# Attention with an expert layer on one core: first x tiles in PSUM, the rare-case flag inside the plan, outputs in another order, no table of rank shifts, longer dense dummies

## The chip, the core and the metric

One core of a Trainium2 chip runs the whole program. The metric is the device time of one execution in microseconds (us), as the median of several. The engines are named as in the profile: PE (TensorE, matrix products, with PEld for its weight loads), DVE (VectorE), ACT (ScalarE), POOL (GpSimd) and SP (SyncE, which issues nearly all DMAs). A name with q behind it (SPq) is an engine's queue. Matrix products write PSUM banks of 512 fp32 columns; DVE and ACT can read them, POOL and DMAs can't.

## What is computed

```python
B, H, S, D = 4, 8, 768, 64            # n_sink 4, window 128
scores = matmul(q, k.T) / sqrt(D)
keep = is_sink | ((rel >= 0) & (rel < window))
a = softmax(where(keep, scores, -1e9))
x = matmul(a, v) -> [3072 tokens, 512]
gate = 1 / (1 + exp(-(x @ w_gate)))   # w_gate, w_val: 512 x 1536
val = x @ w_val
out = (gate * val) @ w_out            # w_out: 1536 x 512
```

Inputs of the expert layer's weights are 64-bit floats. The products of the expert layer keep fp32 accuracy by splitting each operand into a high part (rounded to fp32r) and the rest, and summing three products: high x high, high x rest, rest x high.

## The kernel before

**A planner orders everything.** The kernel builds a list of operations (`plan.op`), each with a priority, one or more engines that could run it with an estimated time, the tiles it reads and those it writes. `Plan.run` then plays a clock: whenever an engine is free, it takes the ready operation with the smallest priority, gives it its buffers, and appends it to that engine's instruction stream. `Tile` is a buffer drawn from a numbered set (`tag`, `bufs`); `plan.over` names sets that share memory, where a later one is given out only once all of the earlier are through. An operation's `slack` delays, in the plan, the moment at which its tiles come free. On PE an operation is *sure* only some time (`SURE` 600 ns, `SURE_D` 1200 ns after a DMA) after its last producer should end.

**Dummies.** When PE finds nothing, `Plan.run` may put in a dummy product (`warm`, of the identity with itself). While the planner's clock is under `DENSE`, operations that aren't sure are held back and a dummy is put in every time; after that an operation that isn't sure may run, and a dummy is put in only when PE's share of work lately is under `FLOOR`.

**Rank shifts.** `RANKS` is a table of 862 numbers. Just before the plan runs, a loop at the end adds to each operation's priority the number that stands for its engine and its group (attention operations by their step u, expert operations by their place in a chunk).

**Attention.** 24 tiles of 128 rows are taken two at a time (12 supertiles), each in four steps of two heads; u counts heads, 0 to 95. `attend` issues for each step: loads of k, q, v; scores on PE into two PSUM banks; masking and the row minimum on DVE (`pick`, `top`, the latter writing a column of `negm_all`), exp on ACT, normalising (`norm`) on POOL or DVE, four transposes on PE, a copy on ACT, a selection on POOL (`split`), and the product with the values on PE (`pv`, `pv_one` for the early steps) into a bank of the set AS (`a`, four banks, used for scores and transposes too). ACT copies that bank to a quarter of x in SBUF (`xr`, one tile for every two steps). After the fourth step `join` adds the sink columns: a PE product of `sk` and `vsp` into a fresh bank, a DVE addition onto xr, then `copy` rounds to `XH` and `rest` takes the difference `XL`, on DVE or POOL.

**Expert layer.** Tiles in `SPILL` go to DRAM for later. The other four supertiles run through `feed` (chunks ci = 0 to 3, 256 rows, 12 slices f of the hidden width) while attention goes on and the weights are decoded from their 64-bit form (`decode`, `weights`). The rest are four wide blocks of 512 rows (`wino`, ci = 4 to 7) that use seven products in place of eight: NP = 6 passes p, each with a gate and a value unit (`Unit`, steps `first` to `fourth`) and `downs`, which splits the hidden tile and queues seven products in the list `coming`. Those are run between the steps of the next pass: one after `first`, two each after `second`, `third` and `fourth`. PE runs the wide blocks in exactly the order in which their operations are listed (`pe_op`). `passing` products go through a rotating bank and are added to one of four accumulators in SBUF (`ACC`, profile name tf); `staying` products accumulate in PSUM over all passes. After the seventh product of the last pass, `merge` combines the accumulators and `emit` writes four outputs, each a DMA of 256 KB. The next block's accumulators are the same four buffers.

**The end.** After `plan.run` come the operations that decide whether the inputs were unusual (`bad`, `count`, `flag`, `total`), a load of that number on every engine, and a branch to `general`, which is not taken here. The last block takes another path through `downs` and `emit` (`last`).

The lines of the loops that matter, beside the functions below:

```python
for i in range(len(OS)): plan.over[f"o{i}", 0] = {("eO", i)}
MX = {3: MS, 2: [MS[0][:, 0:256], MS[1][:, 0:256], MS[1][:, 256:512]]}   # banks of the plain expert products, "m2"
DROPS = ((1, 2, 2, 2), (0, 2, 2, 3)) + ((1, 2, 2, 2),) * 4 + ((0, 1, 2, 4),)
```

In the profile nearly every instruction stands at line 677, since one helper (`InOrder`) records them all; they are told apart by their tiles' names.

## Time and profile before

| | |
|---|---|
| timed runs | 714.39, 716.55, 717.35 us; median 716.55 |
| the profiled execution | 718.86 us, of which 717.1 us are the span from first to last instruction |
| mean granted clock of PE | 0.996 of full speed |
| busy PE / DVE / ACT / POOL | 98% / 79% / 53% / 73% |
| DMA | 152.75 MB, mean 213 GB/s |

The rows below come from one profiled execution; times in them are us from the start of its span, or durations in us, and ns where a row says mean ns. A bracket at the end of a row of the timeline gives how long the engine sat idle before it and what released it. A matmul's busy time is its latency, so products that follow each other overlap in it.

### The profile page before, as it was taken

The page shows a single profiled execution, that of the slowest core. Times are in us where ns is not written, and L with a number is a line of the kernel's source. Part 1 is how long each engine was busy: PE and PEld are TensorE (multiplying, and loading weights), DVE is VectorE, ACT ScalarE, POOL GpSimd, SP SyncE. Part 2 cuts the span into 40 slices and gives each one's busy share as a digit, 9 for nine tenths or more (in the row PEclk, how much of TensorE's full clock was granted, in tenths as well). Part 3 has the DMA queues.
Part 4 walks back from the last instruction along what each step waited for, and adds up shares of the span by engine and source line. Part 5 has one row for each costly group of instructions (what it writes and reads, how often), then busy time and mean ns, then how long its engine had stood idle before and what let it go on. Part 6 is the DMA issues. An engine that isn't in the chain of part 4 may idle for free.

```text
span 717.1 us, 18023 instructions
## 1 busy us (share of the span) xinstructions
PE 700.7 (98%) x6488; PEld 649.7 (91%) x6488; DVE 570.0 (79%) x1296; ACT 381.4 (53%) x1052; POOL 522.2 (73%) x490
## 2 busy tenths in 40 slices
PE   8999899999999999999999999999899999999997
PEld 7778788888887888888999999999899999999996
DVE  8999989989895677875567798668888688886765
ACT  6898867754544565652453454543445444454431
POOL 3889867699997877764477697775768687786651
PEclk9999999999999999999999999999999999999999
DMA  9987879667776888855757656666467756665611
GB/s 291 295 245 257 289 235 311 233 211 251 245 246 193 273 264 264 283 143 173 233 178 227 185 163 202 210 220 186 154 182 216 227 184 176 184 206 183 187 50 64
DMA packets 110609, 152.75 MB, mean 213 GB/s; under 512 B 11060, under 2 KB 69428, under 8 KB 110516
## 3 DMA queue, kind: packets, MB, share of 16 engines
q1 hardware_dynamic: 110512, 151.56, 67.4%
q8 instruction: 52, 0.85, 0.5%
q14 instruction: 41, 0.34, 0.1%
q10 hardware_dynamic: 4, 0.00, 0.0%
HBM read 124.26 MB, written 27.26 MB: 211 GB/s over the span
## 4 chain that ended last, share of the span: by engine, by line
PE 77%; DVE 12%; DMA 4%; issue 3%; ACT 2%; POOL 1%; SPq 0%; DVEq 0%; POOLq 0%; ACTq 0%
PE a L677 38%; PE m L677 24%; PE o L677 15%; DVE tf L677 3%; DMA out_dram<-tf 2%; DVE w L677 2%; DVE a L677 1%; DVE tt L677 1%; DVE P L677 1%; DVE traw L677 1%; DMA wst<-in_moe_w_gate_dram 1%; DMA wst<-wol_d 1%; DVE XH L677 1%; DMA tf<-tw_d 1%; ACT P L677 1%
## 5 line engine op out<-in xcount | busy, mean ns | idle before, releaser
L677 POOL TENSOR_TENSOR tt<-tf,tt 128x512 fp32r<-128x512 f32 x75 | 103.3, 1389 | 26.9 <-ACT tt L677 11.6
L677 ACT ACTIVATE P<-P,negm_all 128x132 f32<-128x132 f32 x176 | 70.0, 399 | 23.7 <-DVE negm_all L677 23.4
L677 POOL TENSOR_SCALAR_AFFINE_SELECT wt<-wt 128x512 f32<-128x512 f32 (+1 forms) x88 | 63.1, 719 | 15.6 <-ACT wt L677 12.4
L677 PE MATMUL o<-woh,graw 128*128 128x512 f32 x192 | 74.1, 410 | 0.2 <-DVE graw L677 0.2
L677 ACT ACTIVATE tf<-a 128x512 f32<-128x512 f32 x49 | 29.3, 599 | 84.3 <-DVE a L677 62.3
L677 PE MATMUL m<-XH,wvh 128*128 128x256 f32 x216 | 61.6, 296 | 0.9 <-ACT traw L677 0.5
L677 ACT CAST tt<-tf 128x512 fp32r<-128x512 f32 x72 | 44.6, 620 | 27.9 <-PE a L677 21.8
L677 PE MATMUL m<-XH,wgh 128*128 128x256 f32 x193 | 56.5, 293 | 2.1 <-DVE traw L677 2.1
L677 PE MATMUL a<-xa,tt 128*128 128x256 f32 x360 | 57.2, 281 | 0.2 <-DVE a L677 0.2
L677 PE MATMUL m<-XH,wvl 128*128 128x256 f32 x204 | 57.4, 281 | 0.0
L677 PE MATMUL m<-XL,wvh 128*128 128x256 f32 x204 | 57.4, 281 | 0.0
L677 PE MATMUL m<-XH,wgl 128*128 128x256 f32 x192 | 54.4, 283 | 0.0
L677 PE MATMUL m<-XL,wgh 128*128 128x256 f32 x192 | 54.3, 283 | 0.0
L677 POOL TENSOR_TENSOR XH<-tf,XH 128x512 fp32r<-128x512 f32 x25 | 34.1, 1364 | 24.0 <-ACT XH L677 21.6
L677 PEld LDWEIGHTS a<-xa,tt 128*128 128x128 f32 x360 | 49.3, 188 | 0.5 <-DVE a L677 0.4
L677 POOL TENSOR_TENSOR XL<-tf,XL 128x512 fp32r<-128x512 f32 x14 | 18.2, 1303 | 41.2 <-ACT XL L677 41.2
L677 POOL TENSOR_TENSOR P<-P,rs 128x528 f32<-128x528 f32 x34 | 42.7, 1256 | 7.1 <-DVE rs L677 2.4
L677 PEld LDWEIGHTS m<-XH,wvh 128*128 128x128 f32 x216 | 40.0, 189 | 7.0 <-issue 2.9
L677 PEld LDWEIGHTS o<-woh,graw 128*128 128x128 f32 x192 | 36.1, 188 | 10.6 <-issue 3.7
L677 DVE TENSOR_TENSOR a<-a,big 128x256 f32<-128x256 f32 x72 | 30.4, 425 | 18.3 <-PE a L677 17.1
L677 PEld LDWEIGHTS m<-XH,wgh 128*128 128x128 f32 x193 | 36.7, 190 | 6.7 <-DVE traw L677 2.9
L677 DVE COPY_PREDICATED a<-tri,a 128x256 f32<-128x256 int32 (+1 forms) x90 | 30.7, 377 | 13.6 <-PE a L677 13.6
(409 smaller groups left out, 2647.1 us busy)
## 6 DMA issues: line engine op xcount, KB each, us to landing
tf<-tw_d SPq DMA_DIRECT2D x96, 256.0 KB, 3.2
wol<-wol_d SPq DMA_DIRECT2D x90, 256.0 KB, 3.5
qkT<-in_k_dram SPq DMA_DIRECT2D x30, 198.0 KB, 4.1
wgh<-tu_d SPq DMA_DIRECT2D x46, 128.0 KB, 2.7
wgl<-tu_d SPq DMA_DIRECT2D x46, 128.0 KB, 2.9
wvh<-tu_d SPq DMA_DIRECT2D x46, 128.0 KB, 2.6
wvl<-tu_d SPq DMA_DIRECT2D x46, 128.0 KB, 3.5
v<-in_v_dram SPq DMA_DIRECT2D x30, 192.0 KB, 3.6
```

Source lines behind the costliest of these rows:

```text
L677: return lambda *a, **kw: tc.keep_in_program_order(op(*a, **kw))
```

## The change

DENSE goes from 8500 to 16000 (ns of the planner's clock). The table RANKS and the loop that adds it are gone. For the first supertile (two tiles of 128 rows, `DIRECT`) the four value products write into two PSUM banks that are kept (`eM`, which is the second m bank, and one of the set AS), `straight` lets the sink product accumulate there, and rounding and difference read the bank; the expert products get the second m bank only after that (`plan.over["m2", ...]`). At the end of the three inner wide blocks the sixth product is run before the fifth, and outputs leave after the third, fifth, sixth and seventh product in place of all after the seventh; an output's DMA holds its tile 1500 ns longer in the plan (`HOLD`). The flag's operations become operations of the plan, behind the last `top` of attention by their inputs and last in priority among attention's; `OUTP` only gives a name to the 0.5.

```diff
--- before.py
+++ after.py
@@ -40,7 +40,7 @@
 FLOOR = 0.85
-DENSE = 8500.0
+DENSE = 16000.0
 HEAT = 7000.0
@@ -78,6 +78,9 @@
 SPLIT = 6
+DIRECT = 1
+HOLD = 1500.0
+OUTP = 0.5
 B_xr = 3
@@ -95,133 +98,6 @@
 BUFS = {}
-RANKS = dict(
...
-)
 
...
@@ -806,6 +683,8 @@
         plan.over[f"o{i}", 0] = {("eO", i)}
+    for i in (1, 2):
+        plan.over["m2", i] = {("eM", 0)}
 
...
@@ -1099,7 +984,7 @@
                     [sc[e]] + [(MASKS, x) for x in ((0,), (1, 4), (2, 4))[min(t0 + t, 2)]],
-                    [(P, (e, t))],
+                    [(P, (e, t)), (NEGM, (u, e, t))],
                 )
@@ -1166,12 +1051,21 @@
 
+        direct = n_of[b, t0] < DIRECT
         if h % 4 == 0:
-            XS.append(Tile(XR_, None, F32, "xr", 3))
+            if not direct:
+                XS.append(Tile(XR_, None, F32, "xr", 3))
+            elif u == 0:
+                XS.append(Tile(MS[1:], None, F32, "eM", 1))
+            else:
+                XS.append(Tile(AS, None, F32, "a", len(AS)))
         xst, c = XS[-1], h // 2 % 2
         sides = [Tile(AS, None, F32, "a", len(AS)) for _ in range(2 - one)]
+        if direct:
+            sides = [xst]
 
@@ -1195,13 +1089,15 @@
 
+        home = c * W if direct else 0
+
         def pv_one():
                     PE.matmul(
-                        sides[0]()[e * D : e * D + D, c0 : c0 + n], lhsT=vt()[:, e, l],
+                        sides[0]()[e * D : e * D + D, home + c0 : home + c0 + n], lhsT=vt()[:, e, l],
                         rhs=w()[:, e].rearrange("p t x y -> p (t x y)")[:, r0 : r0 + n],
-                        start=i == 0, stop=i == len(wide) - 1, skip_group_check=True,
+                        start=i == 0 and not home, stop=i == len(wide) - 1, skip_group_check=True,
                         tile_position=(0, e * D),
@@ -1238,12 +1134,13 @@
                 )],
-                [vt, wt] + list(r), sides + [(xst, c)] + list(w), parts=True,
-            )
-            plan.op(
-                u, [("A", act(W, True), lambda: A.copy(out=xs()[:, c], in_=sides[0]()[:, 0:W]))],
-                [sides[0]], [(xst, c)],
-            )
+                [vt, wt] + list(r), sides + [(xst, c)] * (not direct) + list(w), parts=True,
+            )
+            if not direct:
+                plan.op(
+                    u, [("A", act(W, True), lambda: A.copy(out=xs()[:, c], in_=sides[0]()[:, 0:W]))],
+                    [sides[0]], [(xst, c)],
+                )
             if not one:
@@ -1256,6 +1153,32 @@
         return rear
+
+    def straight(u, g, T, XS, sk, runs):
+
+        W, vs = T * 128, VSP
+        k = g % RING * 128
+        for i, acc in enumerate(XS):
+
+            def add(i=i, acc=acc):
+                for c in range(2):
+                    PE.matmul(
+                        acc()[:, c * W : c * W + W], lhsT=vs()[:, 2 * i + c], rhs=sk(),
+                        start=False, stop=True, skip_group_check=True,
+                    )
+
+            plan.op(u, [("PE", 2 * mac(W), add)], [vs, sk], [acc])
+            x = lambda acc=acc: acc().rearrange("p (c x) -> p c x", c=2)
+            hi, lo = (lambda i=i, z=z: z()[:, 2 * i : 2 * i + 2, k : k + W] for z in (XH, XL))
+            parts = [(2 * i + c, (g + t) % RING) for t in range(T) for c in range(2)]
+            plan.op(
+                u, [
+                    ("A", act(2 * W, True), lambda x=x, hi=hi: A.copy(out=hi(), in_=x())),
+                    ("V", vec(2 * W), lambda x=x, hi=hi: V.tensor_copy(out=hi(), in_=x())),
+                ], [acc], [(XH, p) for p in parts],
+            )
+            rest(u, 2 * W, lo, x, hi, [acc] + [(XH, p) for p in parts], [(XL, p) for p in parts], True)
 
@@ -1297,6 +1220,9 @@
                 runs.append([t])
+        if n_of[b, t0] < DIRECT:
+            straight(u, g, T, XS, sk, runs)
+            return
         for i, xst in enumerate(XS):
@@ -2133,19 +2059,27 @@
         if p == NP - 1:
-            fourth = coming.pop()
-
-            def done():
-                fourth()
-                merge(ci, sums)
-                for n in range(4):
-                    emit(ci, g, n, O[n] if n < 3 else None, sums[n], False)
-
-            coming.append(done)
+            def also(n, *then):
+                product = coming[n]
+
+                def made():
+                    product()
+                    for x in then:
+                        x()
+
+                coming[n] = made
+
+            out_of = lambda n: lambda: emit(ci, g, n, O[n] if n < 3 else None, sums[n], False)
+            order = (0, 1, 2, 3, 5, 4, 6)
+            coming[:] = [coming[x] for x in order]
+            also(2, out_of(0))
+            also(4, lambda: merge(ci, sums), out_of(3))
+            also(5, out_of(2))
+            also(6, out_of(1))
 
 
-        pr = -1000.0 + ci + 1 - 0.5 / NP
+        pr = -1000.0 + ci + 1 - OUTP / NP
         last = ci == len(MT) + WT - 1
@@ -2157,7 +2091,7 @@
     def emit(ci, g, n, bank, acc, last):
-        pr = -1000.0 + ci + 1 - 0.5 / NP
+        pr = -1000.0 + ci + 1 - OUTP / NP
         r = home_of[1][g + n // 2 * 2] * 128
@@ -2186,7 +2120,7 @@
                 in_=ot()[:, 0:512].rearrange("p (j d) -> p j d", j=2),
-            ), [ot],
+            ), [ot], slack=HOLD,
         )
@@ -2248,40 +2182,40 @@
         feeds()
+    one = keep.tile([128, 1], F32, name="one")
+    nc.vector.memset(one, 1.0)
+    flag = keep.tile([1, 4], I32, name="flag")
+    total = keep.tile([1, 1], I32, name="total")
+    count = Tile(AS, None, F32, "a", len(AS))
+
+    def odd_values():
+        V.tensor_reduce(out=bad[:, 0:1], in_=negm_all, axis=AX.X, op=ALU.max)
+        V.tensor_scalar(
+            out=bad[:, 0:1], in0=bad[:, 0:1], scalar1=1.0e8, scalar2=None, op0=ALU.is_gt
+        )
+        for i, (x, y, op) in enumerate(
+            ((win, 1.0, ALU.is_lt), (win, float(WIN), ALU.is_gt), (nsk, float(NS), ALU.is_gt))
+        ):
+            V.tensor_scalar(out=bad[:, i + 1 : i + 2], in0=x, scalar1=y, scalar2=None, op0=op)
+
+    def counted():
+        PE.matmul(count()[0:1, 0:4], lhsT=one, rhs=bad, start=True, stop=True)
+
+    def decided():
+        V.tensor_copy(out=flag, in_=count()[0:1, 0:4])
+        V.tensor_reduce(out=total, in_=flag, axis=AX.X, op=ALU.max)
+
+    plan.op(B * NT * H // 2 + 1.0, [("V", 900, odd_values)], [NEGM], [FLAG])
+    plan.op(B * NT * H // 2 + 1.0, [("PE", 200, counted)], [FLAG], [count])
+    plan.op(B * NT * H // 2 + 1.0, [("V", 400, decided)], [count], [FLAG])
+
     ci = state["ci"]
         wino(ci + i, 4 * i)
-    for o in plan.ops:
-        e, pr = o.ways[0][0][0], o.prio
-        if 0 <= pr < 100:
-            o.prio += RANKS.get(e, {}).get(round(pr * 100), 0.0)
-        elif -1000.5 < pr < -900:
-            o.prio += RANKS.get("m" + e, {}).get(round((pr + 1000) * 12), 0.0)
-        elif 10000 <= pr < 11000:
-            o.prio += RANKS.get("M", {}).get(round((pr - 10000) * 24), 0.0)
     plan.run(WARM, 218.0, warm)
 
-    bad = keep.tile([128, 4], F32, name="bad")
...
-    V.tensor_reduce(out=total, in_=flag, axis=AX.X, op=ALU.max)
     main.close()
     flagged = nc.values_load(total[0:1, 0:1], min_val=0, max_val=512)
```

## Rows read from the trace of the kernel before

**Rows 1.** Page, part 1: busy us, share of the span, instructions.
```profile
PE 700.7 (98%) x6488; PEld 649.7 (91%) x6488; DVE 570.0 (79%) x1296; ACT 381.4 (53%) x1052; POOL 522.2 (73%) x490
```

**Rows 2.** Stretches: length, then busy us (instructions) of PE, PEld, DVE, ACT, POOL.
```profile
0.00:33.65 33.65, 31.03 (x289) 24.66 (x289) 30.31 (x117) 24.02 (x79) 18.87 (x33) 1.00 0.92 297
33.65:100.00 66.35, 64.16 (x591) 52.61 (x589) 62.28 (x196) 57.68 (x184) 56.35 (x57) 0.97 0.79 251
100.00:344.00 244.00, 242.27 (x2581) 212.63 (x2580) 195.32 (x592) 131.42 (x449) 189.01 (x203) 1.00 0.75 238
344.00:711.82 367.82, 363.01 (x3032) 359.76 (x3030) 280.49 (x384) 168.30 (x343) 258.00 (x198) 1.00 0.60 183
```

**Rows 3.** Dummies: their group (busy, mean ns), then two bursts in the timeline.
```profile
L677 PE MATMUL m<-ident 128*128 128x128 f32 x100 | 16.5, 322 | 1.8 <-POOL ident masks.py:199 1.8
...
1.76 4.21 PE L677 MATMUL m<-ident 128*128 128x128 f32 x18 [1.76 <-POOL ident masks.py:199]
...
12.46 2.05 PE L677 MATMUL m<-ident 128*128 128x128 f32 x16
```

**Rows 4.** PE's wait near 87 us, and the stretch after it (granted clock third from last).
```profile
88.80 0.39 PE L677 MATMUL m<-XH,wgh 128*128 128x256 f32 x1 [1.86 <-DVE traw L677]
...
88.00:94.00 6.00, 5.20 (x39) 4.26 (x40) 4.33 (x17) 4.05 (x14) 3.07 (x5) 0.72 0.73 240
```

**Rows 5.** Timeline around the first join: start us, us, engine, line, operation.
```profile
26.84 0.87 PE L677 MATMUL a<-wt,v 128*64 128x256 f32 x8
27.64 0.94 PE L677 MATMUL m<-ident 128*128 128x128 f32 x6
...
30.00 0.69 DVE L677 TENSOR_TENSOR xr<-o,xr 128x512 f32<-128x512 f32 x1
30.21 0.94 PE L677 MATMUL m<-ident 128*128 128x128 f32 x6
...
31.56 1.28 PE L677 MATMUL m<-ident 128*128 128x128 f32 x10
31.58 1.27 POOL L677 TENSOR_TENSOR XL<-xr,XH 128x512 fp32r<-128x512 f32 x1
...
33.65 0.39 PE L677 MATMUL m<-XH,wgh 128*128 128x256 f32 x1
```

**Rows 6.** Prices, from the groups by form: busy us, mean ns, idle before.
```profile
L677 ACT COPY xr<-a 128x256 f32<-128x256 f32 x48 | 17.7, 369 | 10.7 <-PE a L677 10.6
L677 DVE TENSOR_TENSOR xr<-a,xr 128x512 f32<-128x512 f32 x22 | 15.0, 682 | 2.3 <-PE a L677 2.1
L677 DVE TENSOR_TENSOR XL<-xr,XH 128x512 fp32r<-128x512 f32 x2 | 1.4, 714 | 0.0
L677 DVE CAST XH<-traw 128x512 fp32r<-128x512 f32 x4 | 2.1, 527 | 0.7 <-POOL traw L677 0.6
```

**Rows 7.** Timeline of the end, and the last output DMAs (us to landing).
```profile
711.86 0.76 DVE L677 SCALAR_TENSOR_TENSOR tf<-o,tf 128x256 f32<-128x256 f32 x2 [0.73 <-PE o L677]
...
712.31 0.82 SPq L677 DMA_DIRECT2D out_dram<-tf  x2
...
713.72 0.14 DVE L677 TENSOR_REDUCE total<-flag 1x1 int32<-1x4 int32 x1
...
out_dram<-tf SPq DMA_DIRECT2D x2, 128.0 KB, 1.8
```

**Rows 8.** Borders of wide blocks: chain of waits (first row), then timeline.
```profile
454.02 5.05 DMA out_dram<-tf
...
459.09 0.60 ACT L677 ACTIVATE tf<-o 128x512 f32<-128x512 f32 x1 [1.86 <-DMA out_dram<-tf]
...
459.74 0.38 PE L677 MATMUL o<-wvh,XL 128*128 128x256 f32 x1 [1.08 <-ACT tf L677]
...
552.74 0.38 PE L677 MATMUL m<-wvh,XL 128*128 128x256 f32 x1 [0.35 <-ACT tf L677]
...
644.10 0.39 PE L677 MATMUL o<-wvh,XL 128*128 128x256 f32 x1 [0.23 <-ACT tf L677]
```

More of the change, by code (lines that the diff above doesn't have):

```diff
@@ L775 @@
     READY, ready = Fixed(None), iter(range(1000))
+    NEGM, FLAG = Fixed(None), Fixed(None)
     AS = [ps.tile([128, 512], F32, name=f"a{i}") for i in range(B_a)]
@@ L815 @@
     val = keep.tile([128, 2], F32, name="val")
+    bad = keep.tile([128, 4], F32, name="bad")
     nsk, win = val[:, 0:1], val[:, 1:2]
@@ L949 @@
     ))])
+    cleared = []
     for i in range(len(OS) + BUFS["a"]):
@@ L958 @@
         ], w=[x])
+        cleared.append(x)
+    plan.op(SCALP, [("G", 60, lambda: G.memset(bad[:, 3:4], 0.0))], cleared)
     plan.op(SCALP, [("V", 530, scalars)], w=[nums])
@@ L969 @@
     place, home_of, n = {}, ([], []), 0
+    n_of = {}
     for b in range(B):
@@ L974 @@
             place[b, t0] = n in SPILL, len(to)
+            n_of[b, t0] = n
             to += range(b * NT + t0, b * NT + t0 + T)
@@ L1174, in attend @@
         sides = [Tile(AS, None, F32, "a", len(AS)) for _ in range(2 - one)]
+        if direct:
+            assert one and T == 2 and not place[b, t0][0]
+            sides = [xst]
         blocks = []
@@ L1258, in attend @@
         return rear
+    def straight(u, g, T, XS, sk, runs):
+        W, vs = T * 128, VSP
+        assert runs == [[0, 1]]
+        k = g % RING * 128
[17 more added lines that the diff above has]
+            rest(u, 2 * W, lo, x, hi, [acc] + [(XH, p) for p in parts], [(XL, p) for p in parts], True)
     def join(u, b, t0, T, XS, psk):
@@ L2253 @@
         wino(ci + i, 4 * i)
-    for o in plan.ops:
-        e, pr = o.ways[0][0][0], o.prio
-        if 0 <= pr < 100:
-            o.prio += RANKS.get(e, {}).get(round(pr * 100), 0.0)
-        elif -1000.5 < pr < -900:
-            o.prio += RANKS.get("m" + e, {}).get(round((pr + 1000) * 12), 0.0)
-        elif 10000 <= pr < 11000:
-            o.prio += RANKS.get("M", {}).get(round((pr - 10000) * 24), 0.0)
     plan.run(WARM, 218.0, warm)
     wres = {f: [w() if i < 4 else w()[:, 0] for i, w in enumerate(ws)] for f, ws in wres.items()}
-    bad = keep.tile([128, 4], F32, name="bad")
-    V.tensor_reduce(
-        out=bad[:, 0:1], in_=negm_all, axis=AX.X, op=ALU.max
-    )
-    V.tensor_scalar(
-        out=bad[:, 0:1], in0=bad[:, 0:1], scalar1=1.0e8, scalar2=None, op0=ALU.is_gt
-    )
-    for i, (s, x, op) in enumerate(
-        ((win, 1.0, ALU.is_lt), (win, float(WIN), ALU.is_gt), (nsk, float(NS), ALU.is_gt))
-    ):
-        V.tensor_scalar(out=bad[:, i + 1 : i + 2], in0=s, scalar1=x, scalar2=None, op0=op)
-    one = keep.tile([128, 1], F32, name="one")
-    V.memset(one, 1.0)
-    count = AS[0]
-    PE.matmul(count[0:1, 0:4], lhsT=one, rhs=bad, start=True, stop=True)
-    flag = keep.tile([1, 4], I32, name="flag")
-    V.tensor_copy(out=flag, in_=count[0:1, 0:4])
-    total = keep.tile([1, 1], I32, name="total")
-    V.tensor_reduce(out=total, in_=flag, axis=AX.X, op=ALU.max)
     main.close()
```

10 lines of the change are left out of this document (removed), and 115 rows, old and new, of tables (A, G, M, P).

## The prediction, made before the changed kernel ran

> **What bounds the kernel now.** I read the page first: TensorE (PE) is busy 700.7 of 717.1 us, VectorE (DVE) 79% of it, ScalarE (ACT) 53%, GpSimd (POOL) 73% [rows 1]. So a change can only pay by taking something off PE's own time line, and the next view is that time line, cut where its character changes [rows 2]: up to 33.65 us, where the first expert product starts; to 100 us, beside the decoding of the weights; to 344 us, the rest of attention beside plain expert products; to 711.82 us, the four wide blocks. The reader is to take busy from length in each: PE idles 33.65 - 31.03 = 2.62 us in the first, then 66.35 - 64.16 = 2.19, 244.00 - 242.27 = 1.73 and 367.82 - 363.01 = 4.81. From 33.65 to 711.82 us that is 8.73 us in 678: little idle time is left to win. After the last product come 717.10 - 711.82 = 5.28 us of end.
>
> The busy time hides two kinds of waste. One is the dummy products: 100 records, 16.5 us of PE [rows 3]. Two records are one dummy (the product of weights and values shows the same doubling: 4 matmuls in the code, 8 records [rows 5]), so they are 50, and all lie before 33 us. The other is a low clock. The first 9 dummies (18 records) took 4.21 us, 0.47 each, and 8 later ones 2.05 us, 0.26 each [rows 3]: PE starts at about half speed, though the granted clock reads 1.00 there. Later the clock falls in the open: at 86.94 us PE waits 1.86 us for DVE, and from 88 to 94 us the mean granted clock is 0.72 [rows 4], so the lower of the two levels (1.2 against 2.4 GHz) held for part of it. That loses 6 x (1 - 0.72) = 1.7 us more; the event cost 1.9 + 1.7 = 3.6 us. What can be won at all stands on this list: 16.5 us of dummies (4.2 of them before 6 us, when hardly an input is there), 8.7 idle, 1.7 of clock, a part of the 5.3 at the end.
>
> **The change part by part.**
>
> **First tiles in PSUM.** Before, the last of four products of weights and values of the first supertile runs on PE at 26.84 us; ACT copies it to SBUF, DVE adds the sink part (second addition 30.00), ACT rounds, POOL takes the second difference (31.58, 1.27 us long), and the first expert product starts at 33.65 [rows 5]. The change lets the sink product accumulate on the bank where the sum already stands. It removes four ACT copies (4 x 0.37 = 1.5 us of ACT) and two DVE additions (2 x 0.68 = 1.4 us of DVE), and moves a difference from POOL (1.27) to DVE (0.71) [rows 6]. PE keeps its four sink matmuls. Of the chain a copy (0.37) and an addition (0.68) go, and 1.27 becomes 0.71: 1.6 us. What PE does meanwhile is dummies: 0.94 + 0.94 + 1.28 = 3.16 us of them between the two ends of that chain [rows 5], so up to 3.2 us could be filled with expert work. Nothing is won if the other engines are the limit: after 33.65 us DVE is busy 62.28 of 66.35 us and ACT 57.68 [rows 2]. I take the chain's -1.6, with bounds -3.2 and 0. The cost of its own: one of four score banks is held from the third pair's product to the last difference, and half of the expert banks from the first pair's; both are free before an expert product can start, so I put that at nothing. If a score has to wait for the held bank, the gain is gone.
>
> A rule speaks against this part. The rounding would read PSUM. From SBUF DVE rounds 512 columns in 0.53 us; reading PSUM its 512-column additions take 0.68 [rows 6]. The Trainium skill, page "VectorE: DVE Perf Modes", section "Mode 2×_2P — use both read ports for one tensor", says that the doubled fp32 copy rate needs SBUF operands, since PSUM offers one read port. By that two roundings on DVE would cost 2 x 0.15 = 0.3 us more and the part would bring 1.3. The sum below doesn't use it.
>
> **Denser dummies.** Up to 16 us of its own clock instead of 8.5 the planner holds every PE operation whose inputs aren't surely there (0.6 us after the producer, 1.2 after a DMA, by its constants) and puts a dummy in its place. Of PE's 2.62 us idle in the first stretch 1.76 lie before the first dummy [rows 2, 3], so 0.86 at most could be filled, and dummies after 12 us already run at 0.26 each, so no clock is to be won by then. The price is a real operation that comes one hold later: 0 to +1.2 us, mostly beside DVE, which has other work. Bounds -0.86 and +1.2; I take +0.3.
>
> **The flag.** Before, behind the last output piece (DVE 711.86 to 712.62) stand eight DVE operations and a PE product until 713.72 + 0.14 = 713.86; only then do the engines load the flag and branch. The last output DMA is issued until 712.31 + 0.82 = 713.13 and takes 1.8 us to land [rows 7]. After, SP loads the flag right behind its last issue, at 713.13 instead of 713.86: -0.7. If the whole DVE chain counts, -1.24; if the landing near 714.9 sets the end, little: the bound there is 0. In its new place the flag costs DVE about 1.3 us and PE 0.2 (what the same operations take at the end) near 320 us, where DVE is busy 195.32 of 244.00 us [rows 2]: covered; without that cover 1.3. It also holds a score bank, and the wide blocks get the score banks only when it is through; until 344 us PE has plain expert products to do, so this costs nothing unless DVE leaves the flag, last in its priority, for later than that.
>
> **Chunk ends.** At the three inner borders of the wide blocks the outputs leave together, after all seven products. At the worst an output DMA takes 5.05 us (454.02), only then can ACT write the accumulator's next content (459.09), and PE, which needs the bank that ACT reads, has waited 1.08 us; at the two other borders 0.35 and 0.23: 1.66 us [rows 8]. The new order lets the first output go after the third product and the fourth after the fifth, several us of products earlier, and the allowance of 1.5 us makes the plan count on slower landings. Who is late next: SP issues output DMAs between its loads, 0.41 us each [rows 7], in other places but not more of them; two in front of a load that is needed would cost 0.8. I take -1.3, bounds -1.66 and +0.8.
>
> **No rank shifts.** 862 entries that moved groups of operations on all queues go. No instruction is added or removed, but what each engine takes first among the ready is drawn anew, for all of the plan. No row shows the other order. The loss is bounded by the worst stretch in the rows, 3.6 us at 87 us: three more such are +11. The best is that half of the stalls outside the other terms (8.73 - 1.66 = 7.1, with 1.7 of clock 8.8) goes: -4.4. From 100 us on DVE has slack (195 of 244 and 280 of 368 us) and covers much of it; from 33.65 to 100 us DVE, ACT and POOL are busy 94, 87 and 85% [rows 2] and don't. I take some less than half of one event, +1.5.
>
> The sum: -1.6 + 0.3 - 0.7 - 1.3 + 1.5 = -1.8 us. The profiled execution took 718.86 us for a span of 717.1; by the sum it would take 717.1 with a span of 715.3. The timed runs (714.39 to 717.35) have a median of 716.55, 2.3 below it, so the forecast for the median is 714.7.
>
> **The rivals.** **The order helps** (faster): the new order keeps PE fed where it now stalls at 87 us (-3.6), fills all of the 3.2 us of dummies, -1.24 at the end, -1.66 at the borders: -9.7, about 707. For it: all four wastes stand in rows. Against: a new order draws new stalls as well. **Stalls that also cost clock** (slower): with DVE 94% busy between 33.65 and 100 us, the expert products' gate comes late behind attention work on DVE, and each such wait of near 2 us costs 3.6. The other parts bring 3.3, so from the first such event beyond today's on the gain is gone, and from two the kernel is slower beyond doubt; three give 716.55 - 3.3 + 10.8 = 724. For it: the one event there is lies in that stretch. Against: it is only one in 66 us. **The borders don't change** (the change doesn't do what it says): expert products keep a fixed order on PE, and if the accumulators still come free only with a late DMA, the 1.66 us stay: 716. **The held bank**: a score waits for it, and the start loses 1 us where it should win 1.6: 717.3.
>
> **How the numbers follow.** Forecast 0.34, order helps 0.32, clock stalls 0.24, borders 0.06, held bank 0.04. A measurement of this kernel tells about 0.5% (3.6 us) from no change. Faster than 713.0: 0.32 and 0.04 out of the forecast's own spread, 0.36. Slower than 720.1: 0.24 and 0.02, 0.26. Between them 0.38. The forecast alone spans 712 to 718; the range leaves out the far part of either large rival: 706 to 723.
>
> **What would show it.** The first expert product near 32 us with fewer than 100 dummy records before it (first tiles, dummies); no flag operations behind the last output and less than 4.8 us from the last product to the end (flag); no wait of PE for ACT behind an output DMA at the borders (chunk ends); between the first and the last expert product an idle time of PE near 8 us and at most one dip of the granted clock (order). I am wrong if that idle time is above 14 us, if the clock dips three times, or if dummies appear after 34 us.

## The result, and the profile after

The changed kernel takes 709.25 us (median of four executions, 709.08 to 709.57), the kernel before, beside it, 716.65 (714.39 to 717.35). The ratio is 0.9891, with a 95% interval of 0.9868 to 0.9914: 1.1% faster; the forecast was 714.7.

First the page's busy row of after, then its stretches, cut at the same events as [rows 2] (length, then busy us and instructions of PE, PEld, DVE, ACT, POOL, the granted clock, DMA share, GB/s): up to the first expert product at 31.54 us, beside the decoding, beside the rest of attention, the wide blocks up to the last product at 701.45, the end.

```profile
PE 695.0 (98%) x6488; PEld 647.5 (92%) x6488; DVE 570.3 (81%) x1299; ACT 381.0 (54%) x1056; POOL 521.3 (74%) x478
...
0.00:31.54 31.54, 27.90 (x286) 22.87 (x287) 27.23 (x120) 22.67 (x76) 17.75 (x33) 1.00 0.93 301
31.54:100.00 68.46, 68.18 (x648) 56.08 (x647) 62.34 (x196) 56.29 (x185) 60.80 (x61) 1.00 0.82 254
100.00:338.29 238.29, 236.90 (x2527) 208.91 (x2526) 197.62 (x600) 132.28 (x452) 186.88 (x189) 1.00 0.76 242
338.29:701.45 363.16, 362.01 (x3033) 359.68 (x3031) 282.32 (x384) 169.79 (x345) 255.87 (x197) 1.00 0.61 186
701.45:707.40 5.95, 0.00 (x1) 0.00 (x0) 0.76 (x2) 0.00 (x0) 0.00 (x0) 0.88 0.31 99
```

The span falls from 717.1 to 707.4 us, 9.7, and the two tables say where. The first expert product comes 33.65 - 31.54 = 2.1 us earlier. Between the first and the last one PE idles 0.28 + 1.39 + 1.15 = 2.8 us in place of 8.7, so 5.9 are won there, and is busy 667.1 us in place of 669.4, of which 1.7 are the dip of the clock near 90 us that is gone: the stretch of [rows 4] now reads

```profile
88.00:94.00 6.00, 6.00 (x54) 5.27 (x53) 4.89 (x12) 4.85 (x13) 5.22 (x7) 1.00 0.68 219
```

Only the end is longer, 5.95 us for 5.28: 2.1 + 5.9 + 2.3 - 0.7 = 9.7 with rounding. (The profiled execution of before, 718.86 us, lay 2.2 us above its median, that of after, 709.08, at its median; so 9.7 us of span are 7.4 in the medians.)

The start, against [rows 5] (timeline: start, us, engine, line, operation):

```profile
28.07 0.87 PE L553 MATMUL a<-ew,ev 128*64 128x256 f32 x8
28.35 0.56 ACT L553 CAST XH<-m 128x512 fp32r<-128x512 f32 x1
...
28.88 0.51 PE L553 MATMUL a<-sk,vsp 96*128 96x256 f32 x2
...
30.31 0.53 PEld L553 LDWEIGHTS a<-ek,eq 64*64 64x64 f32 x14 [0.37 <-DVE negm_all L553]
...
30.61 0.69 DVE L553 TENSOR_TENSOR XL<-a,XH 128x512 fp32r<-128x512 f32 x1
...
31.54 0.36 PE L553 MATMUL m<-XH,wgh 128*128 128x256 f32 x1
```

The reader is to see that from the last product of weights and values (28.07) to the first expert product are 3.5 us, where they were 33.65 - 26.84 = 6.8: no copy, no addition, and a difference of 0.69 on DVE. (The wait in the PEld row is taken up further down.) The dummies are again 100 records: 98 ahead of the first expert product and two, which are one dummy, at 69 us.

A border of the wide blocks, against [rows 8], and the end, against [rows 7]:

```profile
624.46 1.81 SPq L553 DMA_DIRECT2D out_dram<-tf  x3
...
701.49 0.76 DVE L553 SCALAR_TENSOR_TENSOR tf<-a,tf 128x256 f32<-128x256 f32 x2 [0.73 <-PE a L553]
...
700.79 2.58 SPq L553 DMA_DIRECT2D out_dram<-tf  x3
...
out_dram<-tf SPq DMA_DIRECT2D x2, 128.0 KB, 3.2
```

Three of the outputs of the third wide block are issued between 624.5 and 626.3 us, far ahead of the border, and no product waits for ACT behind an output at any border. At the end no flag operation follows DVE's last output, and yet the end isn't shorter. The last issue ends 1.9 us behind the last product (700.79 + 2.58 = 703.37), where it was 1.3, and the last outputs take 3.2 us to land, where they took 1.8.

What the end waits for shows in the traces of all kernels below. In the six kernels with the flag behind the plan the span ends 3.3 us after the flag is ready and 5.3 us after the last product, the same in each. In the eight traces of kernels with the flag in the plan it ends 1.6 us after the last output has landed, the same in each, and 4.7 to 5.9 us after the last product. With the flag behind the plan the last output had landed 2.6 us before the end, 1 us earlier than the 1.6 that it needs. So the flag did set the end before, and the landing sets it now.

### The profile page after: what moved, and what is told of

Its sections match the earlier page's. It is cut to its first block, busy times and chain, and to the rows that moved or that the text cites. A ratio compares the mean times of both kernels' runs of the same rounds, so it can differ in the third digit from the quotient of the medians.

```text
span 707.4 us, 18014 instructions
## 1 busy us (share of the span) xinstructions
PE 695.0 (98%) x6488; PEld 647.5 (92%) x6488; DVE 570.3 (81%) x1299; ACT 381.0 (54%) x1056; POOL 521.3 (74%) x478
## 4 chain that ended last, share of the span: by engine, by line
## 5 line engine op out<-in xcount | busy, mean ns | idle before, releaser
L553 POOL TENSOR_TENSOR tt<-tf,tt 128x512 fp32r<-128x512 f32 x75 | 105.9, 1422 | 12.8 <-ACT tt L553 5.8
L553 POOL TENSOR_SCALAR_AFFINE_SELECT wt<-wt 128x512 f32<-128x512 f32 (+1 forms) x88 | 65.9, 750 | 16.5 <-ACT wt L553 13.2
L553 ACT ACTIVATE tf<-a 128x512 f32<-128x512 f32 x52 | 31.1, 599 | 79.4 <-DVE a L553 61.5
L553 POOL TENSOR_TENSOR XH<-tf,XH 128x512 fp32r<-128x512 f32 x26 | 36.5, 1404 | 25.9 <-ACT XH L553 25.3
L553 POOL TENSOR_TENSOR XL<-tf,XL 128x512 fp32r<-128x512 f32 x16 | 21.0, 1314 | 44.2 <-ACT XL L553 35.9
L553 DVE CUSTOM_DVE_ANT_0 P<-a,am 128x132 f32<-128x132 f32 x164 | 41.4, 285 | 0.2
L553 PEld LDWEIGHTS a<-wt,v 64*64 64x64 f32 (+1 forms) x832 | 29.7, 133 | 11.2 <-issue 2.8
```

The lines of the kernel that those rows point to most:

```text
L553: return lambda *a, **kw: tc.keep_in_program_order(op(*a, **kw))
```

## The experiments

The question was whether the gain is that of the parts, each by its own row, or that of the new order as a whole, which every part redraws. Five kernels are the kernel after with one part undone, two are the kernel before without its table (one of these with the first tiles in PSUM), four are random orders, two of either kind of parts, and one run repeats the kernel after. Ratios are to the kernel before, run beside each. Where a time lies outside the ranges of both theories, the text says so.

**The table alone.** The kernel before, without it:

```diff
-RANKS = dict(...)
-    for o in plan.ops: ... o.prio += RANKS...
```

> The kernel before with the table of rank shifts and its loop taken out, nothing else. Theory A (the order the table made was the cause of most stalls on PE: idle time 8.7 us and one dip of the clock, 1.7 us): about 711 us (709 to 713), PE idle between the first and the last expert product under 5 us, no wait near 87 us. Theory B (the gain comes from the parts that were put in: first tiles in PSUM, borders, flag): 715 to 720 us, idle of 8 us or more somewhere, since the order is only another draw.

Measured 716.37 us (714.51 to 720.42), ratio 1.0009 (0.9990 to 1.0029). PE's timeline is another one, the time is the same. That refutes theory A; theory B has the time right, with 7.6 us of idle where it named 8 or more. The longest wait at a border, and the stretch behind it:

```profile
641.96 0.41 PE L550 MATMUL o<-wvh,XL 128*128 128x256 f32 x1 [1.75 <-ACT tf L550]
...
642.00:648.00 6.00, 6.00 (x38) 6.00 (x39) 2.81 (x4) 2.95 (x7) 3.08 (x3) 0.72 0.56 170
```

So the table's removal by itself is worth nothing, and a border can cost more than [rows 8] show: 1.75 us of waiting and 6 x (1 - 0.72) = 1.7 of clock.

**The attention part of the table put back into the kernel after.** The shifts of the expert operations stay out.

```diff
+    for o in plan.ops:
+        if 0 <= o.prio < 100: o.prio += RANKS...
```

> The changed kernel with the part of the table back that shifts attention's operations and the decoding (priorities 0 to 100). Theory A: 712 to 715 us, waits of PE return between 32 and 340 us (5 us or more of idle there, where the changed kernel has 1.7). Theory B: 709 to 711 us, idle there under 3 us.

717.02 us (715.33 to 718.30), ratio 1.0012 (0.9995 to 1.0029): the whole gain is gone, with the four other parts in place; that is slower than either theory had. Of 678.18 us between its first and last expert product PE is busy 668.49; the waits stand in the stretch beside attention, as

```profile
100.39 0.38 PE L680 MATMUL m<-XH,wvh 128*128 128x256 f32 x1 [1.18 <-ACT traw L680]
...
170.44 0.50 PE L680 MATMUL o<-woh,graw 128*128 128x512 f32 x1 [1.29 <-POOL graw L680]
```

**Without the first tiles in PSUM.**

```diff
-DIRECT = 1
+DIRECT = 0
```

> The changed kernel with DIRECT 0: the first supertile's x goes through SBUF as before. Theory A (the start gives the 2.1 us by which the first expert product came earlier, and they reach the end): first expert product 1 to 2.5 us later, 710.5 to 711.5 us. Theory B (the other engines limit the time after the start, so that earlier products only wait later): first expert product later by as much, but 709 to 710 us in all.

715.24 us (713.50 to 718.37), ratio 0.9995 (0.9973 to 1.0017). Neither theory had that. The first expert product comes at 34.12 us, 2.6 later than in the kernel after. The other 3.4 us of the 6 lie elsewhere: in the profiled execution (715.83) PE idles 8.2 us between the first and the last expert product, in place of 2.8. The longest shows what these waits are (ACT's rows, then PE's):

```profile
118.30 0.76 ACT L553 CAST zs<-wsx 128x512 f16<-128x512 bf16 x1 [2.60 <-DMA wsx<-in_moe_w_gate_dram]
118.94 0.37 ACT L553 ACTIVATE traw<-m 128x256 f32<-128x256 f32 x1
...
119.36 0.39 PE L553 MATMUL m<-XH,wvh 128*128 128x256 f32 x1 [2.49 <-ACT traw L553]
```

ACT takes its instructions in the planned order, and a cast of weights whose DMA hadn't landed stood ahead of the activation that frees the gate's bank. ACT slept 2.60 us, the activation behind it came late, and PE, in its own order, stood 2.49. In the kernel after the same activation, the twelfth of its kind, comes at 112.24 us, and the product behind it doesn't wait.

**Old chunk ends.**

```diff
-HOLD = 1500.0
+HOLD = 0.0
-            order = (0, 1, 2, 3, 5, 4, 6)  ...  also(6, out_of(1))
+            def done(): fourth(); merge(ci, sums); for n in range(4): emit(...)
```

> The changed kernel with the old order at chunk ends: all four outputs after the seventh product, no allowance on their DMAs. Theory A (the late output DMA holds the accumulator): waits of PE for ACT behind an output DMA return at the three borders, 1 to 2 us in sum, 710.3 to 711.3 us. Theory B (without the table the borders don't wait anyhow): none of these waits, 709 to 709.8 us.

712.68 us (709.87 to 714.18), ratio 0.9952 (0.9932 to 0.9973), slower than either theory had. PE's instructions are the same, one for one, as in the kernel after for the first 4256 of 6488 records, up to 434 us, where the first border begins. So this is the part's own price, with whatever it redraws of the wide blocks: 712.68 - 709.25 = 3.4 us. By the ratios to the kernel before it is (0.9952 - 0.9891) x 716.65 = 4.4, so some 1 us of it is unsure. The profiled execution was the fastest of the seven, and even there a wait of 0.70 us for ACT is back (the slower ones left no trace, but some list a mean clock of 0.996, where the profiled one has 0.999):

```profile
635.74 0.39 PE L553 MATMUL o<-wvh,XL 128*128 128x256 f32 x1 [0.70 <-ACT tf L553]
```

**The kernel after once more.**

> The changed kernel unchanged, beside the next three on one chip. Theory A (its plan keeps PE fed wherever it runs): 709 to 710 us, all runs within 1 us of each other. Theory B (the four runs seen so far were favourable): 710 to 713 us with a spread of 3 us or more, as the kernel before has.

708.96 us (708.72 to 709.47), ratio 0.9898 (0.9861 to 0.9935). Its eight executions in two sets lie within 0.9 us; the 75 of the kernel before beside the experiments lie between 713.67 and 722.50.

**A random order near that of the kernel after**: every priority of attention and of the expert operations up to 0.05 off.

```diff
+    for o in plan.ops:
+        if 0 <= o.prio < 97 or -1000.5 < o.prio < -900:
+            o.prio += 0.1 * (rng.random() - 0.5)
```

> The changed kernel with a random number between -0.05 and 0.05 added to every priority of attention's and the expert layer's operations on engines other than PE's fixed lists: same parts, another order. Theory A (the parts bring the gain, any order without the table does): 709 to 711 us. Theory B (the gain is that of one favourable order): 712 to 717 us, with idle time of PE of 5 us or more between the first and the last expert product.

713.04 us (711.77 to 714.92), ratio 0.9954 (0.9931 to 0.9976). The first expert product stays early (31.88), but PE idles 674.89 - 668.65 = 6.2 us behind it:

```profile
31.88:706.77 674.89, 668.65 (x6219) 625.45 (x6217) 546.94 (x1189) 355.51 (x975) 509.40 (x451) 1.00 0.68 211
...
353.81 0.51 PE L553 MATMUL a<-XH,wvh 128*128 128x256 f32 x2 [1.06 <-DVE tf L553]
```

**The flag behind the plan again.**

```diff
-    plan.op(..., odd_values), plan.op(..., counted), plan.op(..., decided)
+    the same operations after plan.run
```

> The changed kernel with the flag's operations behind the plan again. Theory A (the end is set by the landing of the last output DMA): within 0.5 us of the changed kernel, span from the last DMA issue to the end unchanged near 4 us. Theory B (the chain of flag operations counts): 0.7 to 1.3 us more. If the flag's place in the plan shifts the order of the rest, the time differs by more than that, with stalls of PE to be seen before the end.

708.22 us (707.79 to 708.96), ratio 0.9891 (0.9853 to 0.9928), beside 708.96 of the kernel after. The time is near theory A's, a little beyond its 0.5 us; its reason holds for the kernel after, but not for this one. PE's instructions are the same for the first 3210 of 6488 records, up to 310 us, where the flag's product stands in the kernel after. The end of its timeline:

```profile
699.20 2.87 SPq L553 DMA_DIRECT2D out_dram<-tf  x4
...
702.65 0.14 DVE L553 TENSOR_REDUCE total<-flag 1x1 int32<-1x4 int32 x1
...
out_dram<-tf SPq DMA_DIRECT2D x2, 128.0 KB, 1.7
```

The old place isn't slower. The flag is ready at 702.8 us and sets the end again, at 706.1; the last product comes at 700.76 us in place of 701.45, and the end takes 5.3 us in place of 5.9. The four executions and the four of the kernel after overlap by 0.24 us only, so the flag's new place brings nothing and rather costs 0.7. This kernel is the fastest of all that ran.

Why the landing comes so late with the flag in the plan shows in the DMA's view of both ends: first the kernel after (700 to 703 us), then this one, until its last output has landed (699.2 to 703.5) and behind that (703.5 to 706.1).

```profile
q8 instruction: 1, 0.02, 3.3%
...
out_dram<-tf SPq DMA_DIRECT2D x2, 256.0 KB, 4.2
...
out_dram<-tf SPq DMA_DIRECT2D x2, 256.0 KB, 2.2
...
q8 instruction: 1, 0.02, 3.2%
```

In the kernel after a transfer of instructions (queue q8) runs beside the last outputs; here it comes when they have landed, and the window of the outputs has none. All fourteen traces fall in these two groups: with the flag in the plan the transfer lies among the last outputs, and the last of 256 KB whose landing the trace has takes 3.5 to 4.4 us; with the flag behind the plan the transfer follows the outputs, and that output takes 2.2. That one is the cause of the other is not shown, since no run moves the transfer alone.

**Dense dummies for 8.5 us only.**

```diff
-DENSE = 16000.0
+DENSE = 8500.0
```

> The changed kernel with DENSE back at 8500. Theory A (dummies cost a little): 0.3 us less to 0.3 us more, first expert product earlier by up to 1 us. Theory B (the setting chooses the order of everything after it): a time 3 us or more away from the changed kernel's, by stalls of PE after 32 us, and a first expert product within 1 us of 31.5.

711.42 us (709.88 to 713.29), ratio 0.9933 (0.9908 to 0.9959): 2.2 to 2.5 us slower than the kernel after, which neither theory had. Between the first and the last expert product PE idles 669.23 - 666.04 = 3.2 us, nearly as little as there. The loss stands at the start:

```profile
30.12 0.87 PE L553 MATMUL a<-ew,ev 128*64 128x256 f32 x8
...
31.34 0.48 PE L553 MATMUL a<-sk,vsp 96*128 96x256 f32 x2
...
34.18 0.37 PE L553 MATMUL m<-XH,wgh 128*128 128x256 f32 x1
```

From the last product of weights and values on the chain is short (4.1 us), but that product comes 2.05 us later than in the kernel after: another order ahead of it, with 106 dummy records in place of 98.

**Two random orders of the old parts.** The kernel before without its table, with the random amounts of above, first and second draw.

> The kernel before without its table, with every priority of attention and of the expert products' decoding moved by a random amount of up to 0.05 (first draw): a new order, none of the four other parts. Theory A, the parts carry a good half of the gain whatever the order: this draw stays on the old side, 714 to 720 us, first expert product at 33.3 us or later, a wait of PE for ScalarE of over 1 us at a border of the wide blocks. Theory B, the gain is the luck of one order: this draw is as likely to come out near 711 as at 716, and lands anywhere from 709 to 720.

> The same with a second draw. Theory A: again 714 to 720 us with the first expert product at 33.3 us or later. Theory B: anywhere from 709 to 720; two draws of the old parts and two of the new overlap.

720.89 us (718.14 to 722.70), ratio 1.0048 (1.0022 to 1.0075), and 717.62 us (716.10 to 719.53), ratio 1.0001 (0.9975 to 1.0026). The first product comes at 33.69 and 36.21. The first draw lies just above the ranges of both theories and has no wait for ACT at a border, where theory A wanted one of over 1 us; the second is inside both. The longest wait of the second, and two stretches behind it:

```profile
614.47 0.38 PE L550 MATMUL a<-wgh,tt 128*128 128x256 f32 x1 [1.93 <-POOL tt L550]
...
615.00:618.00 3.00, 3.00 (x20) 3.00 (x20) 1.98 (x2) 1.30 (x4) 2.64 (x3) 0.67 0.35 87
618.00:621.00 3.00, 3.00 (x22) 3.00 (x22) 1.82 (x3) 0.70 (x2) 0.37 (x1) 0.77 0.31 87
```

**The second random order of the new parts.**

> The kernel after with the second draw (the first gave 713.0). Theory A: 710 to 714.5 us, first expert product at 32.9 us or earlier, PE idle 4 to 8 us between the first and the last expert product, no wait of over 0.8 us for ScalarE at a border. Theory B: as likely 715 or more, inside the range of the old parts' draws.

721.68 us (718.63 to 723.93), ratio 1.0078 (1.0051 to 1.0104): slower than the kernel before, 12.4 us slower than the kernel after, with the same parts. The first expert product comes earliest of all, at 30.33, and yet:

```profile
30.33:711.30 680.97, 670.85 (x6235) 627.47 (x6233) 545.90 (x1185) 357.38 (x980) 514.45 (x458) 1.00 0.67 210
...
617.55 0.39 PE L553 MATMUL a<-wgh,tt 128*128 128x256 f32 x1 [2.17 <-POOL tt L553]
...
617.00:620.00 3.00, 2.45 (x20) 2.45 (x21) 1.67 (x3) 1.53 (x4) 2.34 (x3) 1.00 0.55 155
620.00:623.00 3.00, 3.00 (x28) 3.00 (x27) 2.10 (x4) 0.90 (x2) 2.02 (x2) 1.00 0.48 118
```

PE idles 10.1 us behind its first product, and this was the fastest of the ten executions (718.63 us). The expectation that this kernel would stay under 714.5 fell, and with it the theory that the parts carry a good half of the gain whatever the order.

**The first tiles in PSUM alone**, in the kernel before without its table:

```diff
-RANKS = dict(...), and the loop
+DIRECT = 1   # and what belongs to it
```

> The kernel before without its table and with the first two tiles' sums left in PSUM, nothing else of the change. Theory A1, the start is won by the two parts together (tiles in PSUM and 16 us of dense dummies): the first expert product comes at 33.5 us or later, as with either alone (34.12 and 34.18), and the time stays within 2 us of 716.4. Theory A2, the tiles in PSUM win the start by themselves and the run with short dummies had another cause: 31.5 to 32.5 us and some 714 us. Theory B: the first product near 34 and a time anywhere from 709 to 720.

713.28 us (711.06 to 714.96), ratio 0.9946 (0.9922 to 0.9970). The first product comes at 34.14, as with short dummies above and as theory A1 had it; the 3 us against the kernel without table, more than A1 allowed, lie elsewhere. Up to the flag's place (3204 of 6494 records) PE's order is that of the kernel with short dummies, so those two are a second pair for the chunk ends. A border of this one (the chain of waits, ACT, PE, two stretches), then the other's issue and stretch, then the landing times of either kernel's outputs, this one's first; the profiled execution of this one (714.96 us) was the slowest of the ten:

```profile
631.98 6.02 DMA out_dram<-tf
...
638.03 0.60 ACT L553 ACTIVATE tf<-o 128x512 f32<-128x512 f32 x1 [2.88 <-DMA out_dram<-tf]
...
638.68 0.38 PE L553 MATMUL o<-wvh,XL 128*128 128x256 f32 x1 [2.08 <-ACT tf L553]
...
636.00:642.00 6.00, 3.88 (x23) 3.48 (x22) 2.92 (x5) 3.00 (x6) 4.29 (x4) 0.81 0.47 155
642.00:648.00 6.00, 6.00 (x48) 6.00 (x48) 1.39 (x4) 2.13 (x6) 2.22 (x2) 0.91 0.56 177
```

```profile
626.42 1.81 SPq L553 DMA_DIRECT2D out_dram<-tf  x3
...
636.00:642.00 6.00, 6.00 (x53) 6.00 (x52) 4.26 (x5) 3.70 (x10) 5.11 (x5) 1.00 0.67 213
...
out_dram<-tf SPq DMA_DIRECT2D x15, 256.0 KB, 4.2
...
out_dram<-tf SPq DMA_DIRECT2D x15, 256.0 KB, 2.3
```

The old end issues the outputs at 632 to 635.5 us, one takes 6.02 us to land, ACT waits 2.88 for it, and PE 2.08; the new end issues three of them 5.6 us earlier, in a gap between loads (SP issues none from 624.2 to 629.1 us), and nothing waits. They also land sooner: the median of the fifteen is 2.3 us in place of 4.2. In time the pair differs by 713.28 - 711.42 = 1.9 us; by the ratios to the kernel before, whose intervals overlap, it is 0.9, so the size isn't settled by this pair.

**All together.** Waits of PE of over 0.1 us between the first and the last expert product, summed from each trace, by place. A trace is one execution, so its time stands beside the median; the waits are all but 0.3 us of PE's idle time there.

| kernel | median | profiled | first expert product | waits before 340 us | for ACT at borders | others behind 340 us |
|---|---|---|---|---|---|---|
| before | 716.65 | 718.86 | 33.65 | 3.8 | 1.7 | 3.0 |
| after | 709.25 | 709.08 | 31.54 | 1.5 | 0 | 1.1 |
| before, no table | 716.37 | 717.86 | 33.84 | 4.3 | 1.9 | 1.1 |
| same, random 1 | 720.89 | 718.46 | 33.69 | 5.7 | 0 | 3.5 |
| same, random 2 | 717.62 | 719.53 | 36.21 | 2.7 | 1.8 | 3.4 |
| same, first tiles in PSUM | 713.28 | 714.96 | 34.14 | 2.0 | 2.7 | 1.1 |
| after, short dummies | 711.42 | 710.79 | 34.18 | 1.8 | 0 | 1.2 |
| after, flag behind the plan | 708.22 | 707.79 | 31.80 | 1.1 | 0 | 1.0 |
| after, old chunk ends | 712.68 | 709.87 | 31.85 | 1.3 | 0.7 | 1.0 |
| after, no tiles in PSUM | 715.24 | 715.83 | 34.12 | 6.8 | 0 | 1.2 |
| after, attention shifts | 717.02 | 717.65 | 32.88 | 8.3 | 0 | 1.2 |
| after, random 1 | 713.04 | 713.96 | 31.88 | 2.4 | 0 | 3.6 |
| after, random 2 | 721.68 | 718.63 | 30.33 | 5.8 | 0 | 4.2 |

The parts that have a place show in their columns: with the new chunk ends no product waits for ACT at a border, in all kernels that have them (the first random order of the old parts has no such wait either), and tiles in PSUM with the longer dummies bring the first product to 33 us or earlier in all that have both, and in none of the others. The waits before 340 us and the last column are the order's. The random amounts also shuffle the wide blocks, and the last column is higher in all four of those kernels (3.4 to 4.2, against 1.0 to 1.2 in the others and 3.0 in the kernel before), so they are no even sample around their parents. In the first draw the new parts are 720.89 - 713.04 = 7.9 us faster than the old, in the second 721.68 - 717.62 = 4.1 slower. Either draw takes the same random numbers for both, but since the parts change the list of operations, most numbers fall on other operations; these are no matched pairs.

## Why the prediction was right and wrong

The measured time lies within the range, 5.4 us under the forecast, nearest to the first rival, "the order helps". It is that rival that put it inside the range, not the sum, which had 1.8 us of gain where 7.4 came. The terms, one by one:

**First tiles, -1.6: right in its mechanism, short by a little.** Copy, addition and POOL's difference left the chain as costed, and the first product came 2.1 us earlier. The chain itself, from the last product of weights and values, shrank from 6.8 to 3.5 us. What the step missed is that this product isn't fixed: it lay at 26.84 in the kernel before, 28.07 after, 30.12 with short dummies, and there the whole gain of the start was eaten. The time moved by more than the start, by 6.0 us where the part was taken out and by 3.1 where it was put in alone, and that is the order's. One group of scores did wait 0.37 us, at 30.31, until DVE had read earlier scores in a bank of that set, while one of the four was held; whether the hold was the reason isn't shown, and the loss of 1 us of that rival did not come.

The rule that was weighed against this part did come true, without harm. In the kernel after ACT rounded both banks out of PSUM, in 0.56 and 0.58 us; in the two random orders of the new parts DVE rounded one, in 0.69 and 0.68, where it needs 0.53 from SBUF [rows 6]. (The prediction took its 0.68 from additions, which are another operation; the rounding happens to take as long.) The Trainium skill, page "VectorE: DVE Perf Modes", section "Mode 2×_2P — use both read ports for one tensor", says that the faster mode needs operands in SBUF; the traces agree, with 0.15 us each.

**Denser dummies, +0.3: wrong, outside its bounds.** With the first tiles in PSUM they are worth 2.2 to 2.5 us. I costed the dummies and the held operations, but PE's idle time ahead of the first product is 3.6 us with long dummies and 3.9 with short, and dummy records are fewer with long (98 against 106). What I didn't cost is that holding unsure operations back changes which operations come first, and so when the last product of weights and values is done.

**Flag, -0.7: right in what it removes, wrong in what comes next.** The flag's chain did set the end (3.3 us before it, in each of the six kernels that have it there), and without it the landing does, the case for which the bound of 0 was named. In three kernels with the flag in the plan the end is 4.7 or 4.8 us, 0.6 shorter, near the forecast. In the two traces of the kernel after and in three others it is 5.4 to 5.9, longer than before, because the outputs land later than with the flag behind the plan; the prediction took their 1.8 us as given. With the flag behind the plan the kernel is 0.7 us faster, not slower, so the term came out with the other sign.

**Chunk ends, -1.3: right in mechanism, mis-sized.** The two pairs give -3.4 and -1.9 us (by the ratios -4.4 and -0.9); the second contains the flag, so -2.6 without it, if the flag costs 0.7. What the step didn't see is that the outputs, issued in a gap between loads, also land sooner (2.3 us in the median in place of 4.2). One of the four left early before, too: at the first border at 438.80 us, where the next three are issued from 454.02. My bound, -1.66, was the sum of the waits of [rows 8], one execution in which no border was bad enough to lower the clock. Two other kernels with the old ends show a wait of 1.75 and one of 2.08, each with 1.7 us of clock behind it.

**No rank shifts, +1.5: filed in the wrong place.** The table by itself is worth nothing (716.37 for 716.3), but with the other parts in place its attention shifts cost 717.02 - 709.25 = 7.8 us. I took its removal for the only thing that redraws the order, and let the other parts act on a fixed one. Each of them redraws it: a part removed moves waits by up to 5.3 us in places that it doesn't touch (6.8 for 1.5 us before 340 us without tiles in PSUM). The bounds that I gave the new order, -4.4 and +11, were about right for what they were (the kernels with all the new parts span 709 to 722); its value was not +1.5, but some -2.6: of the -7.4 the start has 2.1 and the borders 3.4, and the end lost 0.7, so -7.4 + 2.1 + 3.4 - 0.7 = -2.6. That remainder is an estimate, since the start's 2.1 is taken at its full value, and the run with the earliest start was the slowest. The parts don't add: undone one at a time, tiles, chunk ends and dummies cost 6.0, 3.4 and 2.2, more than the whole gain.

**The rivals.** "The order helps" was put together from the very rows that fell: the stall and the clock near 87 us (3.6), the borders (1.66), a part of the start; its -9.7 is by chance the span's difference to the tenth, since the end brought nothing and other waits went instead. "Stalls that also cost clock" did not happen in this order, but one such stall did in each of three others. The slowest kernel, at 721.68 close to its 724, got there by 10.1 us of waits, with no lower clock in the execution that was profiled. That rival's price was too simple. Of six waits of 1.75 to 2.49 us four were followed by a lower clock and two were not (below). "The borders don't change" is refuted by the borders.

**What would show it.** First product near 32: yes. Under 100 dummy records before it: 98, so hardly fewer. A dummy after 34 us, which was named as a sign of being wrong, did appear: one, of 0.39 us at 69.30, and of no consequence. Under 4.8 us of end: no, 5.95. No wait for ACT at the borders: yes. Idle near 8 us and at most one dip: 2.8, far under it, and none.

**What stays open.** Whether the parts lower the time on the mean over orders isn't settled. Three orders with all the new parts (709, 713, 722; with the attention shifts a fourth, 717) and three with none (716, 721, 718) are too few for a difference of means of some 4 us. Why the order of the changed kernel is as good as it is, no run says; it is one order among those its parts allow, and it reproduces.

## What to carry to other kernels

Where one engine is 98% busy and a planner orders everything, an edit has two effects, its own and that of the order that it redraws, and the second can be several times the first; give that uncertainty to every edit, not to the one that is about order. To price an edit by itself, compare kernels whose instruction order is the same up to the place of the edit, and draw a few neighbouring orders before a gain of 1% is put down to a cause. And a bound taken from one execution's waits is no bound: the same border cost 0.2 to 2.1 us in other executions and kernels, with and without a fall of the clock.

## What the runs showed of the hardware

A single wait of PE near 2 us sometimes lowers its granted clock afterwards and sometimes does not, and its length doesn't tell which. Lower, in stretches of 3 to 6 us with a mean between 0.67 and 0.91, after waits of 1.75 (the kernel without table), 1.86 [rows 4], 1.93 (old parts, second draw) and 2.08 us (tiles in PSUM alone); at 1.00 throughout after 2.17 us (new parts, second draw, rows above) and after 2.49 us (no tiles in PSUM), where the stretches read

```profile
118.00:121.00 3.00, 1.64 (x13) 1.64 (x14) 1.12 (x2) 2.66 (x8) 1.08 (x2) 1.00 1.05 399
121.00:124.00 3.00, 3.00 (x23) 2.61 (x25) 2.14 (x5) 1.49 (x8) 2.22 (x3) 1.00 1.00 337
```

Where it falls, the loss is the same 1.7 us after all four, whatever the wait: 6 x 0.28 twice, 3 x (0.33 + 0.23) and 6 x (0.19 + 0.09). These are single executions, and another of the same kernel may do otherwise: the ten of the new parts' second draw list a mean clock of 0.995 to 0.999 over the whole kernel, and the profiled one is among the highest. The 75 executions of the kernel before list 0.993 to 1.000, median 0.997, and the longest go with the lowest (nine at 1.000 took 714.9 to 716.6 us, three under 0.995 took 718.3 to 722.5); the eight of the kernel after list 0.998 to 1.000, median 0.999. By that some 0.002 x 716 = 1.4 us of the 7.4 is clock, an estimate.

Outputs of the same size take very different times to land in one and the same execution. With tiles in PSUM alone fifteen of 256 KB took 4.2 us in the median, and the one ahead of the wait of 2.08 us took 6.02. In the kernel with short dummies and the new chunk ends, which issues most of them in gaps between loads, the median is 2.3. So in these traces the size of an output doesn't tell when it lands.
